# Thresholded attention and hash routing on one core: another way to turn the last expert's outputs, a split last tile, and another order of the first loads

## The chip, the core and the metric

The kernel runs on one core of a Trainium2 chip. The metric is the device time of one execution in microseconds (us), from the first instruction to the last. The core has a matrix engine (TensorE, PE in the profile, with its weight loads listed as PEld), three engines for elementwise work (VectorE or DVE, ScalarE or ACT, GpSimd or POOL), and SyncE (SP), which here only issues transfers. Each engine runs its own instructions in their order and waits on semaphores for the others. Transfers (DMAs) can be issued by SP, ACT and POOL.

## What is computed

The reference first computes an attention in which only scores close to the row's maximum are kept, and then sends each row to one of eight experts by a hash of its token's number:

```python
scores = scale * np.matmul(q, k.transpose(0, 1, 3, 2))        # 8 x 8 heads, 576 x 576, depth 64
thresh = np.max(scores, axis=-1, keepdims=True) - tau
scores = np.where(scores >= thresh, scores, -1e9)
attn = softmax(scores)                                         # in float32
x = (attn @ v).transpose(0, 2, 1, 3).reshape(4608, 512)
expert = token_ids * 2654435761 % 8
for e in range(8):
    out[expert == e] = np.maximum(x[expert == e] @ w1[e], 0) @ w2[e]   # 512 -> 1024 -> 512
```

Everything is float32.

## The kernel before

**Attention, to about 480 us.** Two heads form a pair; there are 32 pairs, and each pair has five row blocks, so the main loop runs over blocks `n`, with `p, s = divmod(n, 5)`. For block n, `score` (L217) multiplies queries with keys into PSUM, `negate` (L228, DVE) copies the negated scores out and takes their extreme, POOL adds `drop` to it for the threshold (L235), `expo` (L242, ACT) exponentiates, `mask` (L253, DVE) keeps what lies above the threshold and sums it, `turn_w` (L264, PE) turns the weights, `put_wT` (L280 and L285, ACT) copies them back, and `av_part` (L295, PE) multiplies by the values. The order on each engine is written out by hand (`tc.manual_schedule`): the mask of block n-1 stands on DVE behind the negates of block n, and block n-2 is turned beside block n.

Each pair's keys are scaled before use, by 0.125 and by `keep_any`, which is 1 if tau is not negative and 0 otherwise. For pairs from 1 on that is `scale_k` (L197, POOL), and in POOL's order the scaling of pair 1 stands between the threshold of block 0 and that of block 1. For pair 0 it is L539, half on DVE and half on POOL.

**The first loads.** SP issues, in this order: tau (L512), pair 0's keys in two pieces (L173, L174), pair 0's queries, columns 0 to 512, one transfer for each head row half (L170), the token numbers (L515), the values (L190, L194), and then pair 1's keys (L173, L174, L175) and queries. ACT issues the other half of pair 0's keys (L175) and the 64 last query columns (L170). While these come, PE runs 18 transposes of the identity (L631), which change nothing in the result.

**Routing and experts, from about 480 us.** The rows are ranked for each expert while the attention runs, and each expert gets room for 608 rows. An expert e has three full tiles of 128 rows (`kt` = 0, 1, 2; KF = 3) and a last part of 224 rows, which counts as two more tiles. PE computes `gemm1` (L777), then for the last part `gemm2_last` (L804), which leaves the outputs turned, features by rows, in PSUM, and then `gemm2` (L791) for the three full tiles, each into one of two PSUM buffers (`o_ps`); ACT copies each to SBUF (L794), and `put_rows` (L841) stores its rows by an indirect DMA of POOL. All these stores write the one output tensor.

The outputs of the last part must be turned back before they can be stored. For experts 0 to 6 this is `turn_squares` (L810): DVE transposes 32 x 32 squares into `oq` (L815), and SP moves them to their places in `o_last` by 28 transfers of 16 KB each (L823). For expert 7 it is `turn_by_tensor` (L828), called after tile 0: ACT copies the outputs to `oq` (L830), and PE turns them with eight transposes (L836), each group of four copied to `o_last` by ACT (L838). In every expert the two stores of `o_last` stand in POOL's order behind the store of tile 1 and ahead of that of tile 2:

```python
for kt in range(KF):
    gemm2(w2_sb, h_bufs[e % 2], kt, gidx[:, e, kt:kt + 1])
    if (e, kt) == (E - 1, 0):
        turn_by_tensor(oT_ps)
    if kt == 1:
        for k in range(KF, KT):
            put_rows(o_last[:, k - KF], gidx[:, e, k:k + 1])
```

After the experts a loop handles rows that found no room; its count is read from a table at run time, and it is followed by the final waits.

Of the kernel before, what the change touches and what calls it, by code (L numbers as in the profile page):

```python
# [9 lines left out]
FP32 = mybir.dt.float32  # L10
# [3 lines left out]
AF = mybir.ActivationFunctionType  # L14
ALU = mybir.AluOpType
# [5 lines left out]
def kernel(  # L21
# [12 lines left out]
    nc = tc.nc  # L34

    B, H, D, S = qT.shape
    N, DIN = out.shape
# [50 lines left out]
    tau_in = consts.tile([P, 1], FP32, name="tau_in")  # L88
    keep_any = consts.tile([P, 1], FP32, name="keep_any")
    drop = consts.tile([P, 1], FP32, name="drop")  # L90

# [35 lines left out]
    with tc.tile_pool(name="a_q", bufs=1) as a_q, \  # L127
# [29 lines left out]
        def load_pair(p):  # L157
# [23 lines left out]
            for r in range(2):  # L181
                queries(nc.scalar, r, TAIL, S)
            for r in range(2):
                queries(nc.sync, r, 0, TAIL)

# [295 lines left out]
        def scatters():  # L481
# [20 lines left out]
            for _ in range(4):  # L502
# [8 lines left out]

        nc.sync.dma_start(out=tau_in[:],  # L512
                          in_=bass.AP(tensor=tau.tensor, offset=0, ap=[[0, P], [1, 1]]))
        load_pair(0)
# [6 lines left out]
        make_identity(nc, ident[:])  # L521

        nc.vector.tensor_scalar(out=keep_any[:], in0=tau_in[:], scalar1=0.0, scalar2=None,
                                op0=ALU.is_ge)
        nc.vector.tensor_scalar(out=drop[:], in0=keep_any[:], scalar1=-3e38, scalar2=3e38,
                                op0=ALU.mult, op1=ALU.add)
        nc.vector.tensor_tensor(out=drop[:], in0=drop[:], in1=tau_in[:], op=ALU.max)
        for w in w_bufs:  # L530
# [6 lines left out]
        nc.vector.memset(xg_bufs[0][:], 0.0)  # L537
        for j, engine in enumerate((nc.vector, nc.gpsimd)):
            engine.tensor_scalar(out=kts[0][:, j], in0=kts[0][:, j], scalar1=keep_any[:],  # L539
                                 scalar2=SCALE, op0=ALU.mult, op1=ALU.mult)  # L540

# [85 lines left out]
        with tc.manual_schedule():  # L627

            tr = ps_tr.tile([P, 2, 512], FP32, name="tr")
            for _ in range(18):  # L630
                nc.tensor.transpose(tr[:, 0, 0:P], ident[:], ident[:])  # L631
            constants()
            next(pieces)
# [112 lines left out]
    with tc.tile_pool(name="m_x", bufs=1) as m_x, \  # L746
# [40 lines left out]

        def gemm2(w2_sb, h_sb, kt, idx):
            o_ps = ps_o.tile([P, DIN], FP32, name="o_ps")
            for fo in range(FO):  # L790
                nc.tensor.matmul(o_ps[:], lhsT=h_sb[:, fo, FIRST[kt]:FIRST[kt] + P],  # L791
                                 rhs=w2_sb[:, fo, :], start=(fo == 0), stop=(fo == FO - 1))
            o_sb = o_bufs[kt]
            nc.scalar.copy(o_sb[:], o_ps[:])  # L794
            put_rows(o_sb[:], idx)
# [13 lines left out]

        def turn_squares(oT_ps):  # L810


            for i in range(2):
                cols = slice(CO // 2 * i, CO // 2 * i + CO // 2)
                nc.vector.transpose(  # L815
                    out=oq[:, :, cols].rearrange("p b c a -> p c b a"),
                    in_=oT_ps[:, i, 0:CO // 2 * OW].rearrange("p (c b s) -> p c b s", c=CO // 2,
                                                              s=32))
            for h in range(4):
                n = (NB - h + 3) // 4 - KF  # L820
                for g in range(4):
                    for k in range(n):
                        nc.sync.dma_start(  # L823
                            out=o_last[32 * h:32 * h + 32, k].rearrange(
                                "p (c a) -> p c a", c=CO)[:, :, 32 * g:32 * g + 32],
                            in_=oq[32 * g:32 * g + 32, h + 4 * k])

        def turn_by_tensor(oT_ps):  # L828
            oT = oq[:].rearrange("p b c a -> p (b c a)").rearrange("p (c s) -> p c s", c=CO)
            nc.scalar.copy(oT.rearrange("p (i c) s -> p i (c s)", i=2),  # L830
                           oT_ps[:, :, 0:CO // 2 * OW])
            for k in range(KF, KT):
                o_ps = ps_x.tile([P, 2, 512], FP32, name="xT_ps")[:, 0]
                s0, rows = FIRST[k] - FIRST[KF], TROWS[k]
                for co in range(CO):
                    nc.tensor.transpose(o_ps[0:rows, co * P:co * P + P],  # L836
                                        oT[:, co, s0:s0 + rows], ident[:])
                nc.scalar.copy(o_last[0:rows, k - KF], o_ps[0:rows])  # L838

# [24 lines left out]
        with tc.manual_schedule():  # L864
# [4 lines left out]
            for e in range(E):  # L869
# [78 lines left out]
```

## Time and profile before

| | |
|---|---|
| runs | 1006.39, 1008.38, 1009.18 us |
| median | 1008.38 us |
| span of the profiled execution | 1006.4 us |
| mean granted clock of TensorE | 0.993 |
| PE busy in the first of 40 slices of the span | 70% to 80% |
| PE busy in the slices after it | 90% or more |

The profile is of one execution. A line of the timeline gives the start of an instruction in us from the start of the span, its duration, the engine, the line of the kernel, the operation, what it writes and reads with the shape, how many such instructions follow each other, and in brackets how long the engine had been idle before it and what ended that. SPq, ACTq and POOLq are instructions that issue transfers. A matmul in float32 stands as two records: 8 products of 128 x 512 columns are 16 records at L791. The chain of waits follows the last instruction back, step by step, to what released it.

### The profile page before, as it was taken

Reading aid. Unit: us, or ns where it says so; the run is one execution under the profiler, and the core shown is the slowest. Engines: PE = TensorE matmul, PEld = TensorE weight load, DVE = VectorE, ACT = ScalarE, POOL = GpSimd, SP = SyncE. Lnnn points to the kernel's source line nnn. Section 1 sums busy time; section 2 is a strip of 40 time slices with the busy share of each in tenths; the row PEclk is TensorE's granted clock in tenths of the full one; section 3 lists DMA queues with packets and bytes.
Section 4 is the critical chain, followed back from the end, with each engine's and each line's share of the span. In section 5 each row is a group of like instructions: output and inputs, shape, how many; then the busy total and the mean of one; then the engine's idle time right before and its main releaser. Section 6 shows DMA issues by size and latency. Waiting matters only on the chain.

```text
span 1006.4 us, 20417 instructions
## 1 busy us (share of the span) xinstructions
PE 987.5 (98%) x7556; PEld 654.6 (65%) x7556; DVE 516.5 (51%) x1374; ACT 438.1 (44%) x714; POOL 291.4 (29%) x413
## 2 busy tenths in 40 slices
PE   7999999999999999999999999999999999999995
PEld 4666666666666666666766857768577576685762
DVE  7999999999999999994311110010100101110000
ACT  5888888888888888983201000010000000100010
POOL 3233323377766335541321030120210302101001
PEclk9999999999999999999999999999999999999998
DMA  8345544555367677410265353372352723602001
GB/s 181 75 126 140 129 118 112 134 140 118 95 176 184 138 203 194 109 35 25 54 199 165 107 139 108 110 215 90 83 159 88 199 70 113 187 1 49 18 10 37
DMA packets 141571, 116.61 MB, mean 116 GB/s; under 512 B 55908, under 2 KB 115816, under 8 KB 141472
## 3 DMA queue, kind: packets, MB, share of 16 engines
q1 hardware_dynamic: 133248, 96.18, 37.3%
q0 software_dynamic: 7792, 18.91, 6.0%
q8 instruction: 61, 1.00, 0.4%
q14 instruction: 38, 0.31, 0.1%
q10 hardware_dynamic: 432, 0.21, 0.1%
HBM read 81.99 MB, written 22.37 MB: 104 GB/s over the span
## 4 chain that ended last, share of the span: by engine, by line
PE 85%; issue 7%; ACT 2%; DMA 2%; SPq 2%; DVE 1%; POOL 0%; POOLq 0%; DVEq 0%; ACTq 0%
PE sc L777 20%; PE av L295 16%; PE sc L217 14%; PE o_ps L791 12%; PE tr L264 10%; PE sc L804 8%; PE sc L587 3%; SPq L823 2%; PE av L264 1%; ACT w L242 1%; DVE w L253 1%; DMA out_dram<-o_last,gidx 1%; DMA k_sb<-in_k_dram 1%; DMA out_dram<-o,gidx 1%; DVE ns L228 1%
## 5 line engine op out<-in xcount | busy, mean ns | idle before, releaser
L242 ACT ACTIVATE w<-ns,nmx 128x576 f32<-128x576 f32 x288 | 220.4, 777 | 34.9 <-DVE ns L228 34.8
L777 PE MATMUL sc<-xT,w_sb 128*128 128x304 f32 x896 | 230.4, 419 | 0.0
L253 DVE SCALAR_TENSOR_TENSOR w<-ns,thr,w 128x576 f32<-128x576 f32 x288 | 225.6, 815 | 0.0
L777 PEld LDWEIGHTS sc<-xT,w_sb 128*128 128x128 f32 x896 | 170.2, 190 | 61.4 <-issue 3.3
L228 DVE TENSOR_SCALAR_CACHE_REDUCE ns<-sc 128x576 f32<-128x576 f32 x288 | 205.3, 745 | 6.4 <-PE sc L217 5.7
L217 PE MATMUL sc<-k_sb,q 64*128 64x288 f32 (+1 forms) x1280 | 179.1, 423 | 1.3 <-DVE k_sb L539 0.8
L791 PE MATMUL o_ps<-w_sb,h 128*128 128x512 f32 x384 | 167.4, 595 | 0.0
L264 PEld LDWEIGHTS tr<-ident,w 64*128 64x128 f32 x2624 | 107.0, 139 | 88.3 <-ACT wT_b L285 26.1
L235 POOL TENSOR_SCALAR thr<-nmx,drop 128x2 f32<-128x2 f32 (+1 forms) x160 | 101.3, 633 | 173.1 <-DVE ns L228 160.2
L785 DVE TENSOR_SCALAR h<-sc 128x608 f32<-128x608 f32 x28 | 22.2, 792 | 241.4 <-PE sc L777 241.4
L264 PE MATMUL tr<-ident,w 64*128 64x64 f32 x2624 | 139.3, 230 | 2.5 <-ACT wT_a L285 2.0
L794 ACT COPY o<-o_ps 128x512 f32<-128x512 f32 x24 | 14.1, 586 | 276.1 <-PE o_ps L791 276.1
L791 PEld LDWEIGHTS o_ps<-w_sb,h 128*128 128x128 f32 x384 | 73.4, 192 | 88.2 <-issue 88.2
L841 POOL DMA_INDIRECT out_dram<-o,gidx x24 | 23.9, 994 | 327.8 <-ACT o L794 298.4
L217 PEld LDWEIGHTS sc<-k_sb,q 64*128 64x128 f32 (+1 forms) x1280 | 93.1, 177 | 23.5 <-DVE ns L228 9.8
L295 PE MATMUL av<-wT_a,v 128*64 128x320 f32 (+1 forms) x704 | 100.7, 419 | 0.0
L783 ACT ACTIVATE h<-sc 128x608 f32<-128x608 f32 x28 | 19.0, 677 | 182.0 <-PE sc L777 182.0
L804 PE MATMUL sc<-h,w_sb 128*128 128x224 f32 x512 | 98.2, 352 | 0.0
L804 PEld LDWEIGHTS sc<-h,w_sb 128*128 128x128 f32 x512 | 96.9, 190 | 1.1
L285 ACT COPY wT_a<-tr 128x512 f32<-128x512 f32 (+1 forms) x128 | 81.7, 638 | 20.1 <-PE tr L264 19.6
L285 ACT COPY wT_b<-tr 128x512 f32<-128x512 f32 (+1 forms) x128 | 81.2, 634 | 6.7 <-PE tr L264 4.3
L295 PE MATMUL av<-wT_b,v 128*64 128x256 f32 x640 | 83.2, 389 | 0.0
(118 smaller groups left out, 552.9 us busy)
## 6 DMA issues: line engine op xcount, KB each, us to landing
w_sb<-in_moe_w_dram SPq DMA_DIRECT2D x16, 2048.0 KB
q<-in_q_dram SPq DMA_DIRECT2D x62, 288.0 KB
v<-in_v_dram SPq DMA_DIRECT2D x32, 256.0 KB
x_scratch<-xm SPq DMA_DIRECT2D x32, 256.0 KB
xT<-xq SPq DMA_DIRECT2D x84, 80.0 KB
k_sb<-in_k_dram SPq DMA_DIRECT2D x31, 144.0 KB
k_sb<-in_k_dram SPq DMA_DIRECT2D x32, 112.0 KB
o_last<-oq SPq DMA_DIRECT2D x196, 16.0 KB
```

What stands on the lines that cost most here:

```text
L217: nc.tensor.matmul(sc[out_rows, i, 0:S2], lhsT=q_sb[rows, h, q0:q1], rhs=k_sb[rows, h], start=True, stop=True)
L228: nc.vector.tensor_scalar(out=ns[:].rearrange("p (i s) -> p i s", i=2), in0=sc[:, :, 0:S2], scalar1=-1.0, scalar2=None, op0=ALU.mult, op1= ...
L235: nc.gpsimd.tensor_scalar(out=thr[:, 0:j + 1], in0=stats[n][0][:, 0:j + 1], scalar1=drop[:], scalar2=None, op0=ALU.add)
L242: nc.scalar.activation(w, nss[n, j][:], AF.Exp, bias=stats[n][0][:, j:j + 1], scale=-1.0)
L253: nc.vector.scalar_tensor_tensor(out=w, in0=nss.pop((n, j))[:], scalar=stats[n][1][:, j:j + 1], in1=w, op0=ALU.is_le, op1=ALU.mult, accum_ ...
L264: nc.tensor.transpose(dst[:, r, 64 * c:64 * c + 64], src[rows, c0:c0 + P], ident[rows, rows])
L285: nc.scalar.copy(dst, tr[:, :, 0:64 * n_c].rearrange("p r (c q) -> p r c q", c=n_c))
L295: nc.tensor.matmul(av[64 * j:64 * j + 64, g, c0:c1], lhsT=v_sb[:, c, 64 * j:64 * j + 64], rhs=wT[g][:, i, c0:c1], start=(c == 0), stop=stop)
L587: nc.tensor.matmul(h_ps[:, i, 0:CH], lhsT=w1_sb[:, co, fo * P:fo * P + P], rhs=xT_0[:, co, i * CH:i * CH + CH], start=(co == 0), stop=(co ...
L777: nc.tensor.matmul(h_ps[:, i, 0:width], lhsT=w1_sb[:, co, fo * P:fo * P + P], rhs=xT[:, co, i * width:i * width + width], start=(co == 0), ...
L791: nc.tensor.matmul(o_ps[:], lhsT=h_sb[:, fo, FIRST[kt]:FIRST[kt] + P], rhs=w2_sb[:, fo, :], start=(fo == 0), stop=(fo == FO - 1))
L804: nc.tensor.matmul(oT_ps[:, i, c * OW:c * OW + OW], lhsT=w2_sb[:, fo, co * P:co * P + P], rhs=h_sb[:, fo, FIRST[KF]:CAP], start=(fo == ord ...
```

## The change

Five things are changed.

1. Expert 7's last part is turned by `turn_squares` too, and `turn_by_tensor` goes. For expert 7 alone, half of the 28 transfers (those with odd `g`) are issued by ACT, the others by SP. In ACT's order these 14 stand ahead of the copy of tile 0.
2. The last full tile of expert 7 is computed and copied in two column parts, 384 and 128 columns, each in a PSUM buffer of its own. It is still stored by one indirect DMA.
3. SP issues pair 0's queries in four transfers, columns 0 to 128 of both halves and then 128 to 512 of both.
4. tau is loaded by POOL instead of SP; the three small DVE instructions that follow from it move into the hand-written order, and a fourth makes `k_scale`, 0.125 times `keep_any`. Pair 0's keys are scaled by it, one half on DVE and the other on ACT instead of POOL.
5. ACT runs one Exp on a tile of zeros at the start, and PE runs 16 instead of 18 transposes of the identity. In POOL's order the load of tau stands ahead of the last step of making the identity.

```diff
-            for r in range(2):
-                queries(nc.sync, r, 0, TAIL)
+            for c0, c1 in ((0, P), (P, TAIL)):
+                for r in range(2):
+                    queries(nc.sync, r, c0, c1)
...
-        nc.sync.dma_start(out=tau_in[:],
-                          in_=bass.AP(tensor=tau.tensor, offset=0, ap=[[0, P], [1, 1]]))
...
-        for j, engine in enumerate((nc.vector, nc.gpsimd)):
-            engine.tensor_scalar(out=kts[0][:, j], in0=kts[0][:, j], scalar1=keep_any[:],
-                                 scalar2=SCALE, op0=ALU.mult, op1=ALU.mult)
+        nc.scalar.activation(none_f[:], none_f[:], AF.Exp)
...
-            for _ in range(18):
+            for _ in range(16):
                 nc.tensor.transpose(tr[:, 0, 0:P], ident[:], ident[:])
+            nc.gpsimd.dma_start(out=tau_in[:],
+                                in_=bass.AP(tensor=tau.tensor, offset=0, ap=[[0, P], [1, 1]]))
...
+            nc.vector.tensor_scalar(out=k_scale[:], in0=keep_any[:], scalar1=SCALE, scalar2=None,
+                                    op0=ALU.mult)
+            nc.vector.tensor_scalar(out=kts[0][:, 0], in0=kts[0][:, 0], scalar1=k_scale[:],
+                                    scalar2=None, op0=ALU.mult)
+            nc.scalar.activation(kts[0][:, 1], kts[0][:, 1], AF.Copy, scale=k_scale[:])
...
-        def gemm2(w2_sb, h_sb, kt, idx):
+        def gemm2(w2_sb, h_sb, kt, idx, parts=(DIN,)):
...
+            for width in parts:
+                o_ps = ps_o.tile([P, DIN], FP32, name="o_ps")
+                cols = slice(c0, c0 + width)
+                for fo in range(FO):
+                    nc.tensor.matmul(o_ps[:, 0:width], lhsT=h_sb[:, fo, FIRST[kt]:FIRST[kt] + P],
+                                     rhs=w2_sb[:, fo, cols], start=(fo == 0), stop=(fo == FO - 1))
+                nc.scalar.copy(o_sb[:, cols], o_ps[:, 0:width])
+                c0 += width
...
-                        nc.sync.dma_start(
+                        engine = nc.scalar if e == E - 1 and g % 2 else nc.sync
+                        engine.dma_start(
...
-                if e < E - 1:
-                    turn_squares(oT_ps)
+                turn_squares(oT_ps, e)
                 for kt in range(KF):
-                    gemm2(w2_sb, h_bufs[e % 2], kt, gidx[:, e, kt:kt + 1])
-                    if (e, kt) == (E - 1, 0):
-                        turn_by_tensor(oT_ps)
+
+                    gemm2(w2_sb, h_bufs[e % 2], kt, gidx[:, e, kt:kt + 1],
+                          (DIN - P, P) if (e, kt) == (E - 1, KF - 1) else (DIN,))
```

More of the change, by code (lines that the diff above doesn't have):

```diff
@@ L89 @@
     keep_any = consts.tile([P, 1], FP32, name="keep_any")
+    k_scale = consts.tile([P, 1], FP32, name="k_scale")
     drop = consts.tile([P, 1], FP32, name="drop")
@@ L521 @@
         make_identity(nc, ident[:])
[L525 to L529, printed above, removed]
+        none_f = a_st.tile([P, 1], FP32, name="none_f")
+        nc.vector.memset(none_f[:], 0.0)
         for w in w_bufs:
@@ L629 @@
             tr = ps_tr.tile([P, 2, 512], FP32, name="tr")
-            for _ in range(18):
+            for _ in range(16):
                 nc.tensor.transpose(tr[:, 0, 0:P], ident[:], ident[:])
+            nc.gpsimd.dma_start(out=tau_in[:],
+                                in_=bass.AP(tensor=tau.tensor, offset=0, ap=[[0, P], [1, 1]]))
+            nc.vector.tensor_scalar(out=keep_any[:], in0=tau_in[:], scalar1=0.0, scalar2=None,
+                                    op0=ALU.is_ge)
+            nc.vector.tensor_scalar(out=drop[:], in0=keep_any[:], scalar1=-3e38, scalar2=3e38,
+                                    op0=ALU.mult, op1=ALU.add)
+            nc.vector.tensor_tensor(out=drop[:], in0=drop[:], in1=tau_in[:], op=ALU.max)
+            nc.vector.tensor_scalar(out=k_scale[:], in0=keep_any[:], scalar1=SCALE, scalar2=None,
[3 more added lines that the diff above has]
+            nc.scalar.activation(kts[0][:, 1], kts[0][:, 1], AF.Copy, scale=k_scale[:])
             constants()
@@ L786, in gemm1 @@
                                             scalar2=None, op0=ALU.max)
-        def gemm2(w2_sb, h_sb, kt, idx):
[L789 to L794, printed above, removed]
+        def gemm2(w2_sb, h_sb, kt, idx, parts=(DIN,)):
+            o_sb, c0 = o_bufs[kt], 0
+            for width in parts:
[6 more added lines that the diff above has]
+                c0 += width
             put_rows(o_sb[:], idx)
@@ L808, in gemm2_last, with turn_squares @@
             return oT_ps
-        def turn_squares(oT_ps):
+        def turn_squares(oT_ps, e):
             for i in range(2):
@@ L826, in turn_squares @@
                             in_=oq[32 * g:32 * g + 32, h + 4 * k])
[L828 to L838, printed above, removed]
         def put_rows(o_sb, idx):
```

## The prediction

> **What bounds the kernel now.** I read the busy shares first, then the two ends of the run, since the change touches nothing between them.
>
> ```profile
> PE 987.5 (98%) x7556; PEld 654.6 (65%) x7556; DVE 516.5 (51%) x1374; ACT 438.1 (44%) x714; POOL 291.4 (29%) x413
> ```
>
> TensorE (PE) is busy for 98% of the 1006.4 us span: from about 20 us to 957 us its order decides, and a shift made before 20 us is carried through unchanged. The timeline of the tail (start, duration, instruction) shows what decides the end:
>
> ```profile
> 905.51 19.27 SPq L823 DMA_DIRECT2D o_last<-oq  x28
> ...
> 977.15 0.91 ACT L830 COPY oq<-sc 128x896 f32<-128x896 f32 x1
> ...
> 978.11 0.66 PE L836 MATMUL xT_ps<-ident,oq 128*128 128x128 f32 x4 [1.53 <-ACT oq L830]
> ...
> 979.45 1.09 PE L836 MATMUL xT_ps<-ident,oq 128*96 128x128 f32 x4 [0.68 <-ACT o_last L838]
> ...
> 980.33 14.99 PE L791 MATMUL o_ps<-w_sb,h 128*128 128x512 f32 x32
> ...
> 989.39 0.98 POOL L841 DMA_INDIRECT out_dram<-o,gidx  x1 [10.89 <-ACT o L794]
> ...
> 992.34 0.98 POOL L841 DMA_INDIRECT out_dram<-o_last,gidx  x1 [1.98 <-DMA out_dram<-o,gidx]
> ...
> 995.30 0.98 POOL L841 DMA_INDIRECT out_dram<-o_last,gidx  x1 [1.98 <-DMA out_dram<-o_last,gidx]
> 995.40 0.58 ACT L794 COPY o<-o_ps 128x512 f32<-128x512 f32 x1 [6.28 <-PE o_ps L791]
> 999.78 0.98 POOL L841 DMA_INDIRECT out_dram<-o,gidx  x1 [3.50 <-DMA out_dram<-o_last,gidx]
> ```
>
> GpSimd's (POOL's) four last row stores stand in a chain: each waits until the one before has landed, 2.95 us apart, the last 4.48. The last rows are in o_2 at 995.98, yet their store leaves at 999.78. So the end is set by when the chain starts, at 989.39, when o_1 is copied; TensorE's own last matmul has 3.8 us of slack. The windows give TensorE's state while it turns the tiles (busy, ..., granted clock, DMA share, GB/s):
>
> ```profile
> 977.00:980.30 3.30, 1.51 (x8) 1.25 (x9) 0.00 (x0) 1.65 (x3) 0.98 (x1) 0.82 0.21 79
> 980.30:983.00 2.70, 2.70 (x6) 1.23 (x5) 0.00 (x0) 0.58 (x1) 0.00 (x0) 0.59 0.00 0
> ```
>
> The turning costs idle time and then a clock of 0.59. At the front the same timeline shows:
>
> ```profile
> 1.65 1.41 ACTq L170 DMA_DIRECT2D q<-in_q_dram  x2
> ...
> 7.46 0.29 PEld L217 LDWEIGHTS sc<-k_sb,q 64*128 64x128 f32 x2 [0.44 <-DMA q<-in_q_dram]
> ...
> 7.76 0.60 SPq L175 DMA_DIRECT2D k_sb<-in_k_dram  x1
> ...
> 10.99 0.81 POOL L197 TENSOR_SCALAR k_sb<-k_sb,keep_any 128x576 f32<-128x576 f32 x1 [2.23 <-DMA k_sb<-in_k_dram]
> ...
> 11.78 0.31 POOL L235 TENSOR_SCALAR thr<-nmx,drop 128x2 f32<-128x2 f32 x1
> ...
> 12.47 0.81 DVE L253 SCALAR_TENSOR_TENSOR w<-ns,thr,w 128x576 f32<-128x576 f32 x1
> ```
>
> The first scores wait for q, but the mask of row block 1 (L253 at 12.47) needs a threshold that POOL makes only after scaling pair 1's keys, which waits for their load, the third of three, issued at 7.76.
>
> **What the Trainium skill says.** "DMA: Bandwidth & Descriptors", section "Issuing engines are not separate DMA queues": transfers from several engines share the same 16 DMA engines, and issuing from two saves only sequencer time. That is what is wanted here: in expert 6 SyncE (SP) took 19.27 us to issue 28 transfers of 16 KB while the DMA share was 0.11 to 0.31 (windows from 906 to 927). "TensorE: Matmul & The Clock Gate", section "What's actually happening": an idle TensorE is throttled and needs sustained work to get the clock back; the 0.82 and 0.59 above agree. "ScalarE: Activation LUTs", section "What ACT_TABLE_LOAD costs": about 1283 ns; the trace has 1.28 us at 3.09, before any key has landed, so the added dummy Exp only fixes its place.
>
> **The change, part by part.**
>
> *Tail, TensorE.* Expert 7's turn_by_tensor goes: two ACT copies at L838, one at L830, eight transposes. Tile 1's matmuls start where tile 0's end, at 976.58 (969.55 plus 7.03 for 16 records) instead of 980.33: 3.75 us. Sixteen records at full clock take 6.87 (20.60 for 48, chain of waits); the last 32 took 14.99, so 1.25 us more comes back with the clock. o_1 is complete 5.0 us earlier, and its store could leave at 984.4.
>
> *Tail, two queues.* VectorE's two transposes take 1.19 us (904.30 in expert 6), so from 969.72 they end at 970.95. Then SP and ACT issue 14 transfers each. SP's price is 19.27/28 = 0.69. ACT's I take from its two q loads above, 0.70 each; those ran beside SP's issues, with no doubling. In the built program each queue cycles through four completion semaphores and waits for its fourth-last transfer: four issues are 2.8 us, a transfer lands in 1.82 (924.18 in the chain), so this costs nothing. SP ends at 980.6, landing at 982.5, before the first o_last store can leave at 987.4.
>
> ACT's 14 issues stand ahead of tile 0's copy on ACT: 970.95 + 14 x 0.69 = 980.6, a delay from 976.66. Waiting behind it: that copy (0.59), its store, then tile 1's copy. Tile 0's store leaves at 981.5 (0.86 after the copy's start, as at 976.66 to 977.52), so tile 1's may leave at 981.5 + 2.95 = 984.45: just level with 984.4. Tile 2 reuses tile 0's PSUM buffer only at 983.4. So I price the wait at 0.1; below, nothing; above, at 0.85 per issue, 2.2.
>
> *Tail, the column parts.* Tile 2 becomes 384 + 128 columns: 16 x 0.32 (0.429 scaled) = 5.1, then 16 records that the weight load of 190 ns (L791 row) bounds: 3.0, or 1.7 if columns alone bind. TensorE ends at 983.4 + 8.1 = 991.5, the small copy near 992. That is 1.3 us longer than unsplit, hidden, as is any gain from the shorter copy, by the store chain: 984.5, 987.45, 990.4, then 3.37 (the same step in expert 6, 929.83 to 933.20) to 4.48. In the run shown the 4.48 holds a 16 KB instruction fetch on one DMA engine at 996.5, 1.2 us after TensorE's end; now it would fall near 992.8, at the edge of this store. Midway: 994.35. The end follows 6.6 us later (999.78 to 1006.4): 1000.95, so 5.45 less.
>
> *Front.* tau moves from SP to POOL, ahead of ident's select; an indirect store on POOL costs 0.98 and lands 2.69 after its start (977.52), so tau lands near 3.9 instead of 3.6; four small VectorE operations of 0.19 end near 4.7, before the keys at about 5.4 (5.91 less SP's 0.47 for tau). TensorE's warm-up starts near 2.5 instead of 1.61, and 16 transposes at 0.228 last to 6.15: scores start near 6.2 instead of 6.46. ACT scales the second half of the keys (estimate 0.5 us, copies of 512 columns take 0.58) where POOL took 0.68. With q's first 128 columns ahead of the rest, the waits of 0.44 and 0.47 go: VectorE's first negates come about 0.75 earlier.
>
> But SP now issues four q loads, not two (+1.29), less tau (-0.47), so pair 1's last key load is issued 0.7 to 0.8 later. POOL's threshold had 0.38 us of slack before 12.47 (11.78 + 0.31 against 12.47), so block 1's mask starts about 0.3 later, and VectorE, busy without a gap from there to 24 us, hands this on to TensorE. Bounds: -0.75 if the keys land no later, +0.8 if SP also has to wait on semaphores. I take +0.3.
>
> Sum against this execution's 1006.4: -5.45 + 0.3 = -5.15. It belongs to the median run, timed at 1008.38, so 1003.2.
>
> **The rivals.** *Dear ACT issues (slower).* The place is ACT between 970.95 and tile 0's copy. Break-even in the tail: tile 1's store must leave by 989.39, so tile 0's by 986.44, ACT free by 985.6: 1.05 per issue. For it: SP's xT<-xq transfers took 1.28 each at 859.91; against: a 2 MB weight load ran beside those, and none is left in expert 7. At 1.28: free at 988.9, stores at 989.7, 992.7, 995.6, 998.6, then 1002.5, end 1009.1, plus 0.3: +3.0, or 1011.4.
>
> *The front pays too.* If the key load hides, -0.75, and the fetch misses the chain, -6.0: 1001.6. For it: the DMA engines are near full from 5 to 8 us, so pair 1 may have been waiting for bandwidth, not for its issue. Against: their share is 0.8 from 8 to 10 us.
>
> *Half is lost.* ACT at 0.85 per issue and +0.8 in front: tail -3.3, sum -2.5, or 1005.9, no difference that can be measured. For it: ACT's issues of 0.72 and 0.757 beside SP's at the start; against: its third took 0.62.
>
> *That the change doesn't do what it says* I exclude: in the built program the transposes are gone and ACT holds 14 issues ahead of the copy.
>
> **How the numbers follow.** Chances: forecast 0.58, front pays 0.20, half lost 0.15, dear issues 0.07. What can be told from no change is 0.3%, or 3.0 us. Faster: the first two and 0.01 of the third, 0.79. Same: the rest of the third, and 0.02 of the fourth, at prices between 1.05 and 1.28: 0.16. Slower: 0.05. The range goes from the second rival less 0.8 of scatter (the runs shown spread over 2.8) to the third plus 0.7: 1000.8 to 1006.6.
>
> **What would show it.** Tail: no gap before tile 1, full clock, stores near 984.5, 987.5, 990.4, 994; ACT's issues near 0.69 each, and tile 0's copy at 980.6. Front: pair 1's scaling near 11.7 and a VectorE gap before the mask at 12.8. The forecast is wrong if an ACT issue costs over 0.85, if the o_last stores wait for the squares, or if the shift in front is not carried to TensorE.

## The result, and the profile after

| | before | changed |
|---|---|---|
| median of 6 runs, us | 1008.38 (1006.39 to 1010.61) | 1002.88 (1001.9 to 1004.55) |
| ratio, with its 95% interval | | 0.9948 (0.9931 to 0.9965) |
| span of the profiled execution, us | 1006.4 | 1001.3 |
| start T of expert 7's tile 0 on PE | 969.55 | 969.10 |
| from T to the end of the span | 36.85 | 32.2 |

The changed kernel is 5.5 us faster; the profiled spans differ by 5.1. By the trace, 4.65 us of that lie behind T, in the tail, and 0.45 ahead of it. Of the 4.65, 4.35 come from an earlier store of tile 1 and 0.5 from a shorter last step of the stores (3.97 instead of 4.48); the way from the last store to the end is 0.2 longer. The busy shares of the changed kernel, first part of its page:

```profile
PE 983.8 (98%) x7562; PEld 653.9 (65%) x7562; DVE 517.7 (52%) x1378; ACT 436.9 (44%) x714; POOL 291.7 (29%) x413
```

They look as before, with 3.7 us less on PE; nothing on this line tells where the end comes from. The timeline of the tail does (start, duration, instruction; L802 is gemm2, L804 its copy, L826 VectorE's turning, L835 the squares, L841 the row stores):

```profile
969.10 20.84 PE L802 MATMUL o_ps<-w_sb,h 128*128 128x512 f32 x64
...
969.30 1.18 DVE L826 STREAM_TRANSPOSE oq<-sc 128x448 f32<-128x448 f32 x2 [11.31 <-PE sc L815]
...
970.50 9.22 SPq L835 DMA_DIRECT2D o_last<-oq  x14
970.51 9.62 ACTq L835 DMA_DIRECT2D o_last<-oq  x14
...
980.24 0.58 ACT L804 COPY o<-o_ps 128x512 f32<-128x512 f32 x1 [26.47 <-DMA o_last<-oq]
...
981.10 0.98 POOL L841 DMA_INDIRECT out_dram<-o,gidx  x1 [47.63 <-ACT o L804]
...
983.07 0.59 ACT L804 COPY o<-o_ps 128x512 f32<-128x512 f32 x1 [2.25 <-PE o_ps L802]
984.59 0.98 POOL L841 DMA_INDIRECT out_dram<-o,gidx  x1 [2.50 <-DMA out_dram<-o,gidx]
987.54 0.98 POOL L841 DMA_INDIRECT out_dram<-o_last,gidx  x1 [1.97 <-DMA out_dram<-o,gidx]
...
989.97 0.27 ACT L804 COPY o<-o_ps 128x128 f32<-128x128 f32 x1 [1.26 <-PE o_ps L802]
990.52 0.98 POOL L841 DMA_INDIRECT out_dram<-o_last,gidx  x1 [2.00 <-DMA out_dram<-o_last,gidx]
994.49 0.98 POOL L841 DMA_INDIRECT out_dram<-o,gidx  x1 [2.99 <-DMA out_dram<-o_last,gidx]
```

PE now works through all three tiles, 64 records in 20.84 us without a gap. The last of its results is in SBUF at 990.24 (989.97 plus 0.27), but the last store leaves at 994.49. So the chain of row stores still sets the end. It only starts earlier: the store of tile 1 leaves 15.49 us after T, and before it left at 19.84. In brackets behind tile 1's store (984.59) stands what held it: not its own copy, done at 983.66, but the landing of the store of tile 0, which left late because ACT had 14 issues (9.62 us) ahead of tile 0's copy.

The timeline of the front (L219 scores, L199 scaling of the keys, L237 threshold, L255 mask):

```profile
6.30 2.89 PE L219 MATMUL sc<-k_sb,q 64*64 64x288 f32 x16
...
7.60 0.76 DVE L230 TENSOR_SCALAR_CACHE_REDUCE ns<-sc 128x576 f32<-128x576 f32 x1 [1.95 <-PE sc L219]
...
8.62 0.60 SPq L176 DMA_DIRECT2D k_sb<-in_k_dram  x1
...
11.64 0.75 POOL L199 TENSOR_SCALAR k_sb<-k_sb,keep_any 128x576 f32<-128x576 f32 x1 [2.86 <-DMA k_sb<-in_k_dram]
...
12.37 0.58 POOL L237 TENSOR_SCALAR thr<-nmx,drop 128x2 f32<-128x2 f32 x2
...
12.71 0.82 DVE L255 SCALAR_TENSOR_TENSOR w<-ns,thr,w 128x576 f32<-128x576 f32 x1 [0.40 <-POOL thr L237]
```

Pair 1's last key load is issued 0.86 us later than before, its keys are scaled 0.65 later, and the mask of row block 1 waits 0.40 us for POOL's threshold and starts 0.24 later. The scores do start earlier, but VectorE's first negate begins at 7.60, where it was 7.58. These are single executions: with one and the same front the mask of block 1 can stand 0.9 us apart in two of them, as e1 below shows, so the 0.24 alone proves no delay. What does hold in all profiles is the later scaling: 11.62 to 12.33 with the changed loads, 10.99 and 10.69 with the old ones.

### The profile page after: what moved, and what is told of

The parts are those of the page before. It is cut to its first block, busy times and chain, and to the rows that moved or that the text cites. A ratio compares the mean times of both kernels' runs of the same rounds, so it can differ in the third digit from the quotient of the medians.

```text
span 1001.3 us, 20487 instructions
## 1 busy us (share of the span) xinstructions
PE 983.8 (98%) x7562; PEld 653.9 (65%) x7562; DVE 517.7 (52%) x1378; ACT 436.9 (44%) x714; POOL 291.7 (29%) x413
## 4 chain that ended last, share of the span: by engine, by line
PE 87%; issue 6%; SPq 2%; DMA 2%; ACT 1%; DVE 1%; POOL 0%; POOLq 0%; ACTq 0%
PE sc L784 20%; PE av L297 17%; PE sc L219 15%; PE o_ps L802 12%; PE tr L266 10%; PE sc L815 8%; PE sc L579 3%; SPq L835 2%; PE av L266 1%; DMA out_dram<-o_last,gidx 1%; DMA out_dram<-o,gidx 1%; ACT w L244 1%; PE xT_ps L596 0%; PE sc L596 0%; ACT wT_a L287 0%
## 5 line engine op out<-in xcount | busy, mean ns | idle before, releaser
L255 DVE SCALAR_TENSOR_TENSOR w<-ns,thr,w 128x576 f32<-128x576 f32 x288 | 225.4, 814 | 0.4 <-POOL thr L237 0.4
L219 PE MATMUL sc<-k_sb,q 64*128 64x288 f32 (+1 forms) x1280 | 179.2, 426 | 0.6 <-DVE ns L230 0.4
L802 PE MATMUL o_ps<-w_sb,h 128*128 128x512 f32 (+2 forms) x400 | 166.2, 575 | 0.0
L237 POOL TENSOR_SCALAR thr<-nmx,drop 128x2 f32<-128x2 f32 (+1 forms) x160 | 101.8, 637 | 176.7 <-DVE ns L230 163.4
L804 ACT COPY o<-o_ps 128x512 f32<-128x512 f32 (+2 forms) x25 | 14.2, 569 | 274.5 <-PE o_ps L802 248.1
L802 PEld LDWEIGHTS o_ps<-w_sb,h 128*128 128x128 f32 x400 | 74.9, 190 | 86.8 <-issue 84.7
L841 POOL DMA_INDIRECT out_dram<-o,gidx x24 | 23.9, 996 | 324.0 <-ACT o L804 291.4
L219 PEld LDWEIGHTS sc<-k_sb,q 64*128 64x128 f32 (+1 forms) x1280 | 93.0, 179 | 22.9 <-DVE ns L230 9.7
```

The lines of the kernel that those rows point to most:

```text
L219: nc.tensor.matmul(sc[out_rows, i, 0:S2], lhsT=q_sb[rows, h, q0:q1], rhs=k_sb[rows, h], start=True, stop=True)
L237: nc.gpsimd.tensor_scalar(out=thr[:, 0:j + 1], in0=stats[n][0][:, 0:j + 1], scalar1=drop[:], scalar2=None, op0=ALU.add)
L255: nc.vector.scalar_tensor_tensor(out=w, in0=nss.pop((n, j))[:], scalar=stats[n][1][:, j:j + 1], in1=w, op0=ALU.is_le, op1=ALU.mult, accum_ ...
L802: nc.tensor.matmul(o_ps[:, 0:width], lhsT=h_sb[:, fo, FIRST[kt]:FIRST[kt] + P], rhs=w2_sb[:, fo, cols], start=(fo == 0), stop=(fo == FO - 1))
```

## The experiments

The experiments were timed in three groups (e1 to e4, e5 to e8, e9 to e11), each on one chip and beside the kernel before, which took 1011 to 1012 us there. In their profiles T lies between 971.9 and 978.1 us; the changed kernel itself, timed again (e9), has 974.55 instead of 969.10, and its tail is as it was. So times are compared as ratios to the kernel before in the same group, and the tails by times counted from T in each profile. The theory: the chain of row stores sets the end; it starts when tile 1's store may leave, and the front adds next to nothing. The rivals were that ACT's issues decide, that the front pays, and that the column split or TensorE's earlier end is what pays. All diffs are against the changed kernel; all times in the table are us after T.

| kernel | PE's end | stores, in their order | end of span | ratio (95%) |
|---|---|---|---|---|
| before | 25.77 | 7.97, 19.84, 22.79, 25.75, 30.23 | 36.9 | 1 |
| changed | 20.84 | 12.00, 15.49, 18.44, 21.42, 25.39 | 32.2 | 0.9948 (0.9931 to 0.9965) |
| e1 tail only | 20.84 | 12.34, 15.79, 18.74, 21.69, 25.38 | 32.1 | 0.9961 (0.9949 to 0.9974) |
| e2 front only | 24.4 | 7.98, 18.48, 21.44, 24.42, 29.02 | 35.8 | 1.0007 (0.9996 to 1.0018) |
| e3 one queue | 20.84 | 7.97, 15.13, 21.75, 25.05, 28.44 | 35.25 | 0.9997 (0.9988 to 1.0005) |
| e4 no split | 20.76 | 12.01, 15.49, 18.45, 21.44, 25.25 | 32.1 | 0.9951 (0.9931 to 0.9971) |
| e5 copy on VectorE | 20.84 | 8.09, 14.84, 17.79, 20.78, 25.14 | 31.9 | 0.9966 (0.9953 to 0.9978) |
| e6 stores early | 20.84 | 8.09, 13.43, 16.38, 19.77, 23.25 | 30.1 | 0.9942 (0.9926 to 0.9958) |
| e7 scaling later | 20.84 | 12.01, 15.48, 18.43, 21.42, 25.52 | 32.3 | 0.9957 (0.9941 to 0.9972) |
| e8 all on ACT | 30.46 | 20.89, 24.36, 27.32, 30.3, 35.15 | 42.0 | 1.0057 (1.0041 to 1.0072) |
| e9 changed again | 20.84 | 12.02, 15.5, 18.45, 21.45, 25.14 | 31.95 | 0.9961 (0.9947 to 0.9975) |
| e10 first tile first | 20.84 | 8.09, 11.28, 14.24, 17.63, 21.42 | 29.0 | 0.9928 (0.9914 to 0.9941) |
| e11 busy | 20.84 | 8.09, 11.37, 14.33, 17.72, 21.42 | 29.1 | 0.9965 (0.9952 to 0.9979) |

The order of the stores is tile 0, tile 1, the two of the last part, tile 2; in e6, e10 and e11 it is tile 0, the two of the last part, tile 1, tile 2.

### e1 and e2: the two ends alone

e1 keeps the changed tail and takes the first loads of the kernel before; e2 is the reverse. The core of e1:

```diff
-            for c0, c1 in ((0, P), (P, TAIL)):
-                for r in range(2):
-                    queries(nc.sync, r, c0, c1)
+            for r in range(2):
+                queries(nc.sync, r, 0, TAIL)
...
+        nc.sync.dma_start(out=tau_in[:],
+                          in_=bass.AP(tensor=tau.tensor, offset=0, ap=[[0, P], [1, 1]]))
...
+        for j, engine in enumerate((nc.vector, nc.gpsimd)):
+            engine.tensor_scalar(out=kts[0][:, j], in0=kts[0][:, j], scalar1=keep_any[:],
+                                 scalar2=SCALE, op0=ALU.mult, op1=ALU.mult)
```

and of e2:

```diff
-                turn_squares(oT_ps, e)
+                if e < E - 1:
+                    turn_squares(oT_ps)
                 for kt in range(KF):
-
-                    gemm2(w2_sb, h_bufs[e % 2], kt, gidx[:, e, kt:kt + 1],
-                          (DIN - P, P) if (e, kt) == (E - 1, KF - 1) else (DIN,))
+                    gemm2(w2_sb, h_bufs[e % 2], kt, gidx[:, e, kt:kt + 1])
+                    if (e, kt) == (E - 1, 0):
+                        turn_by_tensor(oT_ps)
```

> The changed tail alone, with the first loads as before. Theory 1 (the chain of GpSimd's row stores sets the end, and its start comes forward): from 5.4 to 4.7 us less than before, with tile 1's store near 984.5 to 985. Rival (the front pays for 0.45 of the 5.1 us): 4.6 us less. In the profile of the front, the mask of block 1 starts near 12.47 as before.

> The changed first loads alone, with the tail as before. Theory of the prediction (the later mask of block 1, near 12.7, is carried through VectorE to TensorE): 0.2 to 0.3 us more than before. Rival 1 (the delay is absorbed before 30 us, and the rest is scatter between executions): 0 within 0.5 us. Rival 2 (the front pays): 0.5 to 0.8 us less.

The tail alone gives 0.9961, the front alone 1.0007 (-0.4 to +1.8 us of 1011). So the gain is the tail's; that the front pays more than 0.4 us is excluded by the interval. Its predicted cost of 0.3 and a cost of nothing are both inside the interval, and are not told apart. e1's time (3.9 us less, between 2.6 and 5.2) and its tail (4.8 us shorter) agree with the 4.7 to 5.4 expected. Its mask of block 1 does not: it was expected near 12.47, as before, and stands at 13.39 with no wait at all:

```profile
13.39 0.81 DVE L254 SCALAR_TENSOR_TENSOR w<-ns,thr,w 128x576 f32<-128x576 f32 x1
```

Pair 1's keys had been scaled early, at 10.69. The trace's record of the granted clock starts with full clock at 10.6 us there and at 6.3 in the kernel before, and the negates came later (the first at 8.14 instead of 7.58). In e2 the mask is late for the other reason, the keys, as these lines of its timeline show:

```profile
12.33 0.75 POOL L199 TENSOR_SCALAR k_sb<-k_sb,keep_any 128x576 f32<-128x576 f32 x1 [3.85 <-DMA k_sb<-in_k_dram]
...
13.40 0.82 DVE L255 SCALAR_TENSOR_TENSOR w<-ns,thr,w 128x576 f32<-128x576 f32 x1 [1.61 <-POOL thr L237]
```

Here the same wait costs VectorE 1.61 us where it was 0.40 in the changed kernel: the second negate came early (7.98), the keys late, and all that was won was waited away again.

### e3: one queue for the squares

```diff
-                        engine = nc.scalar if e == E - 1 and g % 2 else nc.sync
+                        engine = nc.sync
```

> As the changed kernel, but SyncE issues all 28 transfers of the squares, and ScalarE none. Theory 1: the squares land near 990.5 instead of 981.3, so the first store of o_last leaves near 990.8 instead of 987.5 and the end comes 2.5 to 3.5 us later than in the changed kernel; tile 0's copy starts near 976.2 instead of 980.2. Rival (TensorE's removed idle time is the gain, the stores only follow): no difference to the changed kernel.

Ratio 0.9997: with one queue no gain is left in the time, though PE ends at the same 20.84 us. The timeline of its tail:

```profile
975.95 18.12 SPq L835 DMA_DIRECT2D o_last<-oq  x28
...
989.68 0.98 POOL L841 DMA_INDIRECT out_dram<-o,gidx  x1 [6.18 <-ACT o L804]
...
996.30 0.98 POOL L841 DMA_INDIRECT out_dram<-o_last,gidx  x1 [5.64 <-DMA o_last<-oq]
...
1002.99 0.98 POOL L841 DMA_INDIRECT out_dram<-o,gidx  x1 [2.40 <-DMA out_dram<-o_last,gidx]
```

SP issues 28 transfers in 18.12 us, so the squares land after tile 1's store has, and the first store of the last part waits 5.64 us for them. It leaves at T + 21.75 instead of 18.44. TensorE ends 4.9 us earlier than before, but the first store of the last part leaves only 1.0 us earlier (21.75 against 22.79), the profile's tail is 1.6 us shorter, and the interval of the ratio allows a gain of 1.2 us at most. So TensorE's earlier end alone is worth little here, and the two queues are needed. It agrees with what the Trainium skill says in "DMA: Bandwidth & Descriptors", section "Issuing engines are not separate DMA queues" (only time on the sequencer is saved): that time is 18.12 us on one queue against 9.22 and 9.62 side by side. The page calls it usually small beside the transfer; here it was what counted. The profile's tails differ by 3.1 us, the ratios of e3 and e4 by 4.6 (give or take 2); the two agree within that.

### e4: no column split

```diff
-                          (DIN - P, P) if (e, kt) == (E - 1, KF - 1) else (DIN,))
+                          (DIN,))
```

> As the changed kernel, but tile 2 of the last expert in one part of 512 columns. Theory 1 (the store chain hides TensorE's end and the last copy): no difference, within 0.3 us in the tail of the profile; o_2's store leaves 3 to 4 us after o_last's second. Rival (TensorE's end counts): 0.3 us more, the longer copy (0.58 instead of 0.27).

Without the split the ratio is 0.9951, the stores leave at the same times, and PE ends 0.08 us earlier. The split does nothing to the time: the last copy is 0.27 us with it and 0.58 without, and it has about 4 us of slack ahead of its store.

### e8: all 28 transfers on ACT

```diff
-                        engine = nc.scalar if e == E - 1 and g % 2 else nc.sync
+                        engine = nc.scalar if e == E - 1 else nc.sync
```

> As the changed kernel, but ScalarE issues all 28 transfers of the squares: its issues cost twice as much, which is the prediction's slower rival made real. Theory 1: tile 0's copy at 20.7 us from the start of tile 0's matmuls, stores at 21.5, 24.7, 27.7, 30.7 and 34.3, end near 41, 8 to 9 us more than the changed kernel and 3 to 5 us more than the kernel before. Rival (ScalarE's queue is off the path): as with one queue on SyncE, an end at 35.3.

This doubles the wait that the slower rival was built on. The timeline:

```profile
973.35 18.50 ACTq L835 DMA_DIRECT2D o_last<-oq  x28
...
992.60 9.79 PE L802 MATMUL o_ps<-w_sb,h 128*128 128x384 f32 x32 [6.77 <-ACT o L804]
992.82 0.98 POOL L841 DMA_INDIRECT out_dram<-o,gidx  x1 [56.72 <-ACT o L804]
...
1007.08 0.98 POOL L841 DMA_INDIRECT out_dram<-o,gidx  x1 [3.86 <-DMA out_dram<-o_last,gidx]
```

Ratio 1.0057, slower than the kernel before. ACT comes to tile 0's copy only after 18.50 us, tile 0's store leaves at 20.89, PE stands 6.77 us because tile 2 needs the PSUM buffer that this copy frees, and the tail ends 9.8 us later than the changed kernel's (8 to 9 were expected; the last step was 4.85 instead of 3.6). So the rival's mechanism is real. Only its price was not there: an ACT issue costs 18.50/28 = 0.66 here and 9.62/14 = 0.69 in the changed kernel, below its break-even of 1.05.

### e5: tile 0's copy on VectorE

```diff
-        def gemm2(w2_sb, h_sb, kt, idx, parts=(DIN,)):
+        def gemm2(w2_sb, h_sb, kt, idx, parts=(DIN,), on_vector=False):
...
-                nc.scalar.copy(o_sb[:, cols], o_ps[:, 0:width])
+                if on_vector:
+                    nc.vector.tensor_copy(o_sb[:, cols], o_ps[:, 0:width])
+                else:
+                    nc.scalar.copy(o_sb[:, cols], o_ps[:, 0:width])
...
-                          (DIN - P, P) if (e, kt) == (E - 1, KF - 1) else (DIN,))
+                          (DIN - P, P) if (e, kt) == (E - 1, KF - 1) else (DIN,),
+                          on_vector=(e, kt) == (E - 1, 0))
```

> As the changed kernel, but tile 0 of the last expert is copied by VectorE, which is idle then, instead of standing behind ScalarE's 14 issues. Times are counted from the start of tile 0's matmuls in the last expert (969.10 in the changed kernel's profile; its stores follow at 12.0, 15.5, 18.4, 21.4 and 25.4 us, its end at 32.2). Theory 1 (the store of tile 1 waits for the store of tile 0, which waits for the issues): stores at 8, 14.8, 17.8, 20.7, 24.4, end at 31.4 to 31.6, 0.6 to 0.8 us less. Rival (the issues on ScalarE are hidden, as priced at nearly nothing in the prediction): no difference, within 0.2 us.

This takes ACT's 14 issues out of tile 0's way. The timeline:

```profile
979.98 0.69 DVE L805 COPY o<-o_ps 128x512 f32<-128x512 f32 x1 [5.74 <-issue]
...
987.70 0.98 POOL L844 DMA_INDIRECT out_dram<-o,gidx  x1 [5.76 <-ACT o L807]
...
998.00 0.98 POOL L844 DMA_INDIRECT out_dram<-o,gidx  x1 [3.38 <-DMA out_dram<-o_last,gidx]
```

Tile 1's store now waits for its own copy alone and leaves at T + 14.84 instead of 15.49. So the wait on tile 0's store costs 0.65 us in the changed kernel. But the end is only 0.3 us earlier (0.6 to 0.8 were expected), and the ratio, 0.9966, shows no gain: the last step of the chain grew from 3.97 to 4.36 us. What lies in that step is taken up below.

### e6, e7, e10: the order of the stores, and the front's wait

e6 is e5 with the two stores of the last part placed ahead of tile 1's; e7 is the changed kernel with pair 1's keys scaled one step later, behind the thresholds on POOL; e10 has both, and issues the squares of the first tile of the last part before those of the second.

```diff
-                    if kt == 1:
+                    if kt == (0 if e == E - 1 else 1):
```

```diff
-                if s == 1 and p + 1 < NP:
+                if s == (1 if p else 2) and p + 1 < NP:
                     scale_k(p + 1)
```

```diff
-            for h in range(4):
-                n = (NB - h + 3) // 4 - KF
-                for g in range(4):
-                    for k in range(n):
+            for k in range(KT - KF):
+                for h in range(4):
+                    if k >= (NB - h + 3) // 4 - KF:
+                        continue
+                    for g in range(4):
```

> As the run before, and the two stores of o_last stand ahead of tile 1's store in the last expert. Theory 1 (one chain of stores, each waiting for the landing of the one before, sets the end): stores from the start of tile 0's matmuls at 8, 12.5 (the squares have landed), 15.5, 18.5 to 19, and o_2's at 21.5 to 22.5, when its copy is done or just after; end at 28.3 to 29.3, about 3 us less than the changed kernel. Rival (each store only needs its data, the order does not matter): as the run before, 31.5.

> As the changed kernel, but GpSimd scales pair 1's keys behind the threshold of block 1 instead of ahead of it. Theory (the mask of block 1 waits for the keys of pair 1): the mask of block 1 starts when VectorE has negated block 2, 0.3 to 0.8 us earlier, near 12.0 to 12.3 instead of 12.71. Whether this reaches the end: if carried, 0.3 to 0.8 us less in the time; if absorbed before 30 us, no difference.

> The changed kernel with tile 0's copy of the last expert on VectorE, the stores of o_last ahead of tile 1's, the squares of the first o_last tile issued ahead of those of the second, and pair 1's keys scaled behind block 1's threshold. Theory 1 (the chain of stores): stores from the start of tile 0's matmuls at 8.1, 11 to 11.4, 14 to 14.8, 17 to 18.2, and 21.4 to 21.7, when o_2 is copied; end near 28.5, 3.5 us less than the changed kernel, and 0.4 us less in front if that is carried. Rival (a store's own way to the end is longer when another is still landing): 1.5 us less or below.

e6 shortens the tail from 32.2 to 30.1 us and gives 0.9942. Here a store of the last part leaves while PE still computes tile 1, but this store waits 4.36 us for the squares. It leaves at T + 13.43 where 12.5 was expected, and the end misses the expected 28.3 to 29.3 by about 1 us. Issuing the first tile's squares first makes that wait short in e10. The timeline of e10 (tile 0's copy is made by VectorE, and the view names VectorE's queue as what held its store, at 981.86):

```profile
975.18 9.83 ACTq L839 DMA_DIRECT2D o_last<-oq  x14
...
981.86 0.98 POOL L845 DMA_INDIRECT out_dram<-o,gidx  x1 [47.29 <-DVEq L898]
985.05 0.98 POOL L845 DMA_INDIRECT out_dram<-o_last,gidx  x1 [2.21 <-DMA o_last<-oq]
...
988.01 0.98 POOL L845 DMA_INDIRECT out_dram<-o_last,gidx  x1 [1.98 <-DMA out_dram<-o_last,gidx]
991.40 0.98 POOL L845 DMA_INDIRECT out_dram<-o,gidx  x1 [2.41 <-DMA out_dram<-o_last,gidx]
...
995.19 0.98 POOL L845 DMA_INDIRECT out_dram<-o,gidx  x1 [2.80 <-ACT o L807]
```

The chain starts at T + 8.09, and the last store is released by its own copy (ACT, L807): now TensorE's end sets when it leaves, by about 0.3 us, since the store before landed at 994.11 and a store of a full tile follows 0.77 us behind such a landing (last section). The tail is 29.0 us, not the expected 28.5: the last store takes 7.6 us to the end instead of 6.8, with an instruction fetch in it, as told below. Timed beside the changed kernel (e9), e10 has 0.9928 (0.9914 to 0.9941) against 0.9961 (0.9947 to 0.9975): the intervals do not meet, and e10 beats both kernels, the changed one by about 3.3 us (0.0033 of 1012). The tail accounts for about 3 of them; a share of e7's edit in the rest cannot be told apart.

e7 does what it was to do in its own stage, as its timeline shows:

```profile
10.41 0.81 POOL L237 TENSOR_SCALAR thr<-nmx,drop 128x2 f32<-128x2 f32 x1 [1.63 <-DVE ns L230]
...
12.32 0.82 DVE L255 SCALAR_TENSOR_TENSOR w<-ns,thr,w 128x576 f32<-128x576 f32 x1
```

The threshold no longer stands behind the keys, and the mask starts with no wait, 0.39 us earlier than in the changed kernel. Yet 0.9957 cannot be told from it, and ACT's copy near 25 us stands at 24.82 against 25.15. What happens between 13 and 25 us is the next question.

### e9 and e11: the half clock between 15 and 24 us

> The changed kernel itself, beside the two that follow, on their chip. Its ratio to the kernel before: 0.993 to 0.997, as measured first. In the tail the same steps from the start of tile 0's matmuls in the last expert: stores at 12.0, 15.5, 18.4, 21.4 and 25.2 to 25.5, end near 32.2. In the front the mask of block 1 between 12.7 and 13.4, and a window of half clock somewhere between 15 and 24 us.

> As the run before, and 42 transposes of the identity more, into a PSUM tile not yet used, stand in TensorE's order of blocks 1 to 5, to be done in its waits. Theory (a window of half clock between 15 and 24 us, brought on by TensorE's waits from 9 to 20 us, costs the front more than the loads do): no such window, and the copies near 25 us come 1 to 2 us earlier, counted from the mask of block 1; 1 to 2 us less at the end. Rival (the added transposes delay what stands behind them, or the window comes anyway): no difference, or up to 1 us more.

In the changed kernel the copies near 25 us stand where they did before (25.15 against 25.20), though the mask of block 1 is 0.24 later. The windows of the changed kernel (from:to, length, busy us of PE, PEld, DVE, ACT, POOL, then granted clock, DMA share, GB/s):

```profile
18.00:20.00 2.00, 1.48 (x18) 0.80 (x18) 2.00 (x7) 1.90 (x4) 0.72 (x1) 0.68 1.21 235
20.00:22.00 2.00, 2.00 (x18) 1.41 (x16) 1.81 (x7) 1.57 (x3) 0.63 (x1) 0.50 1.00 241
```

and of the kernel before:

```profile
20.00:22.00 2.00, 2.00 (x14) 1.15 (x14) 2.00 (x6) 1.46 (x3) 0.73 (x1) 0.50 0.82 206
22.00:24.00 2.00, 2.00 (x20) 1.23 (x18) 2.00 (x7) 1.36 (x2) 1.53 (x4) 0.66 0.98 216
```

Each has a stretch at half clock of about 3.4 us, at another place: 18.7 to 22.1 and 20.0 to 23.4. In e1 it is 20.8 to 24.3, in e7 18.9 to 22.3, in e9 20.2 to 23.7, in e8 14.8 to 18.2; in e2, e3, e4 and e6 it lasts 6.8 us; in e5, e10 and e11 there is none. In the clock records of these ten traces the stretch starts 6.83, 10.24 or 13.65 us after the first record of full clock, two, three or four times 3.41, and that first record itself lies anywhere from 5.9 to 10.6 us. The Trainium skill, "TensorE: Matmul & The Clock Gate", section "What's actually happening", says that the clock is halved after an idle window of about 3.4 us; the lengths of 3.41 and 6.83 agree with that window. A wholly idle window stands ahead of none of these stretches: TensorE was busy for 52% to 62% of the 3.41 us before them, and in e5 61% (15.47 to 18.88) brought none. So the traces don't tell what share of work would avoid it. From the mask of block 1 to that copy it takes 12.44 us in the changed kernel, 12.73 before, 13.0 to 13.6 with the long stretch, 11.5 to 12.0 with none (e5, e10) or an early one (e8). So a difference of 1 to 2 us in this hand-on goes with the stretch, more than the front's shift of 0.24. e9, which is the changed kernel once more, has 12.71.

e11 is e10 with transposes added that keep TensorE busy in that stage:

```diff
+        def keep_busy(n):
+            for _ in range(2 if 1 <= n <= 5 else 0):
+                nc.tensor.transpose(av[:, 1, 384:512], ident[:], ident[:])
```

It is called at five places of each of the blocks 1 to 5, which makes 50 transposes (the expectation says 42). There is no half clock, but e10 had none either. The copy near 25 us stands at 29.13 where e10 has 23.80, the end is 4.4 us later, and the ratio is 0.9965. Neither expectation foresaw so much (at most 1 us more); the rival's direction is right: the added transposes stand in the way of the work. The 5.3 us lost at that copy are 4.4 at T, so most of a large delay in this stage is carried to the end. That the half-clock stretch costs the 1 to 2 us stays an agreement between profiles, since e10 had no such stretch to begin with.

## Why the prediction was right

Predicted were 1003.2 us and faster; measured were 1002.88. That it came within 0.3 us is luck, since two errors stand against each other: in the profiles the tail gave 4.65 where 5.45 were predicted, and ahead of T 0.45 were gained where 0.3 were to be lost. The 0.45 is put down to no edit: e5 and e8, with the same front and on the same chip, differ by 0.9 in T.

**The bound.** Right: the chain of row stores sets the end and TensorE's own end has slack. e3 shows it best, with the same PE end and no gain in the time.

**TensorE in the tail.** Right: no gap, full clock, tile 1's copy at T + 13.97.

**Two queues.** Right in size: 0.66 (SP) and 0.69 (ACT) per issue against 0.69 predicted for both. Tile 0's copy starts at T + 11.14, predicted 11.05; its store at 12.0, predicted 11.95.

**The wait of tile 1's store.** This is the term that was mis-sized: "so tile 1's may leave at 981.5 + 2.95 = 984.45 ... So I price the wait at 0.1". The step from tile 0's store to tile 1's is 3.49 us, not 2.95, and the wait costs 0.65 (15.49 in the changed kernel against 14.84 in e5). It was inside the bounds given, nothing to 2.2. The 2.95 was read from steps into a store of the last part; steps into a store of a full tile that waited for the store before were 3.39 or more in every tail. The prediction had such a step before it, the 3.37 of expert 6, and used it for the last store alone. Where the 0.5 us lie is shown in the last section.

**The rest of the chain.** Two steps of 2.95 and 2.98, predicted 2.95 each; the last 3.97, predicted 3.95 as a midway between 3.37 and 4.48; then 6.8 to the end, predicted 6.6. That the last step came out as predicted rests on where the fetch fell. With 0.54 from tile 1's store, 0.03, 0.02 and 0.2 these make up the 0.8 that the tail fell short.

**The column parts.** Right that they are hidden (e4). Of the two bounds given for the narrow part the lower held: its 16 records take 1.74 us, as if the columns alone bound them. The split cost 0.08 us at TensorE's end, not 1.3.

**The front.** The times up to the mask came out as predicted: scores at 6.30 (6.2), scaling of pair 1 at 11.64 (11.7), mask at 12.71 (12.8), with VectorE's gap. For the scaling the mechanism holds in every profile with this order of loads; that the mask came out is partly chance, by e1's 13.39 with the old front. tau came some 0.7 us later than priced (its first reader starts at 4.65), at no cost, since the scores follow the 16 transposes directly. Two things failed. "VectorE's first negates come about 0.75 earlier" did not hold in this execution: the first came at 7.60, while the trace's record of full clock starts only at 8.5 us (6.3 before); the second came 0.23 earlier in the changed kernel, and 0.8 to 1.4 earlier in e2, e3, e4, e6, e9 and e10. And "VectorE, busy without a gap from there to 24 us, hands this on to TensorE" is not seen in a delay of some tenths: between 13 and 25 us the executions differ by more. The prediction had named this as a sign of being wrong ("if the shift in front is not carried to TensorE"), so its +0.3 stands unproven: the time neither confirmed nor refuted it (e2).

**The rivals.** Dear ACT issues: the mechanism is shown by e8; the price is below its break-even in every run. The front pays too: excluded beyond 0.4 us by e2. Half is lost: its issue at 0.85 did not come about; its 0.8 in front lies inside e2's interval and is not excluded.

## What to carry to other kernels

Where stores wait on one another, read the order and the steps of that chain before the engine that feeds it: earlier results are worth little if the chain's next link, here transfers issued by one queue, comes late (e3), and a chain that starts with what is ready first was worth more than half as much again as the change (e10, with tile 0's copy on VectorE: about 3 us of tail beside 4.65). Splitting a burst of issues over a second engine pays if what stands behind them on that engine can wait or can be moved elsewhere, and the price of each step has to be taken from a step of the same kind. At the start of a kernel a shift of some tenths of a us can't be carried through on paper while the granted clock there differs from run to run.

## What was not expected of the hardware

**The last step of the chain and an instruction fetch.** In the stretch of the changed kernel from 990.5 to 993.8 us the DMA view shows, beside the store, one instruction fetch (queue and kind, packets, MB, share of 16 engines):

```profile
q0 software_dynamic: 80, 0.18, 15.4%
...
q8 instruction: 1, 0.02, 2.7%
```

and in the same step of e3, from 999.6 to 1002.4 us, there is the store alone:

```profile
q0 software_dynamic: 80, 0.18, 17.6%
```

The fetch (991.16 to 992.57, on one of the DMA engines) starts 1.2 to 1.8 us after TensorE's end, here and in the other profiles. Fifteen of the sixteen landings of the changed kernel's store fall between 992.76 and 993.12, one at 993.72. Over the profiles the step from the last part's second store to the store of a full tile behind it is 3.39 us with no fetch in it (e3, e6, e10, e11), 3.69 to 3.97 where the fetch starts 0.39 to 0.64 after the store's issue (e1, e4, e9, changed), and 4.10 to 4.85 where it starts 1.22 to 1.38 after (e7, before, e5, e2, e8). In all nine with the fetch in that store its last landing comes 1.13 to 1.15 us after the fetch's end, wherever that lies. By this agreement e5's earlier chain ended hardly earlier, and 0.5 us of the change's own gain hang on it (4.48 before, 3.97 now). In e3 the fetch falls into the store ahead, and that step is the one exception below (3.30). In e10 and e11 it falls into the very last store, one landing comes about 0.8 us behind the other fifteen, and the end follows 7.6 us after the issue instead of 6.6 to 6.8. It is an agreement over thirteen profiles; no run moved the fetch by itself.

**Steps of unequal length.** Where a store waited only for the one before, a step into a store of the last part was 2.95 to 3.00 us (but 3.30 in e3), and one into a store of a full tile 3.39 or more. The chain of waits of the changed kernel shows where the difference lies (start, duration, what passed):

```profile
981.10 2.71 DMA out_dram<-o,gidx
...
983.84 0.02 POOLq L841
983.86 0.51 issue
984.37 0.03 POOLq L841
...
984.59 0.07 POOL out_dram L841
984.66 2.64 issue
987.30 0.03 POOLq L841
...
987.54 0.98 POOL out_dram L841
```

Tile 0's store has landed at 983.82, and tile 1's leaves 0.77 us later: POOL passes a short instruction at 983.84, and 0.51 us go by before its next one at 984.37. Tile 1's own store lands at 987.27; POOL goes on at 987.30, and the last part's first store leaves 0.27 us after the landing. In all thirteen profiles the two gaps are 0.77 us and 0.26 to 0.27 us wherever a store waited for the one before alone, while a landing with neither a fetch nor the squares' transfers beside it takes 2.6 to 2.7 us from the issue for both kinds. So the extra 0.5 us lie on POOL, between the landing and the next store, and not in the transfer. What POOL does in them is open.

**Listed loads.** A weight load in float32 is listed with 0.19 us, yet 16 records of 128 columns, each with its load, passed in 1.74 us, 0.11 each. So here the listed duration of a load is no bound on how close products follow each other.
